# Separate PSUM banks for the two halves of one down-projection pair, two tail loads in place of one, and new engine orders, in a pre-norm linear-attention and GEGLU block

## The chip, the core and the metric

The kernel runs on one core of a Trainium2 chip. The metric is device time in microseconds (us), the median of repeated runs. One more execution was taken with the hardware profiler; its rows are quoted with the names the profile uses: PE is TensorE (PEld its weight loads), DVE VectorE, ACT ScalarE, POOL GpSimd, and SP SyncE, which here only issues DMAs.

## What is computed

One block of a transformer on x of 2048 rows by 448 columns in bfloat16: linear attention with 16 heads of 28, then a gated MLP of inner width 1792, each behind a layer norm and added to its input.

```
x = A_x;  h  = x + A(layernorm(x));  h2 = h + B(layernorm(h))
A: q, k, v = split(x @ wqkv);  phi(t) = where(t > 0, t + 1, exp(t)) + 1e-6
   kv = sum_s phi(k) v^T;  z = sum_s phi(k);  o = phi(q) kv / (phi(q) z + 1e-6);  return o @ wo
B: return (gelu(x @ w_gate) * (x @ w_up)) @ w_down
```

## The kernel before

**Tiles and stages.** The rows are cut into 16 tiles of 128, two tiles make a pair. The contraction over 448 columns is done as three blocks of 128 rows and a tail of 64 rows, padded with zeros to 128 (memsets, L364).

*Stage one*: for each tile, layer-norm statistics on DVE (`bnst1_t` L412, `bnag1_t` L413), the reciprocal root on ACT (`ln1_t` L419, `rstd1_t` L421), the normalised tile (`normD_t` L434 on DVE for tiles 0 to 3, `normP_t` L452 on POOL for the others), its transpose (for tiles 0 to 3 on PE, `tr0_t` and `tr1_t` L442, copied out of PSUM by ACT L447 and DVE, `evxD_t` L449; for the others a DMA transpose, L454), and the projections `k_t` and `q_t` (four matmuls each, L468; the fourth contracts the tail block). `k_t` is followed by `ek_t` (ACT, L479), `ck_t` (DVE, L480), `pk_t` (DVE, L481, the last reader of the projection's bank) and the accumulation `pt_t` (L487). The projections go round four PSUM banks in the order of the list SEQ (K0 K1 Q0 K2 K3 Q1 ...): `q_1` gets the bank of `k_1`, so it waits for `pk_1`.

*Stage two* makes the attention's output for each pair (`a2_pair`): some DVE and POOL work, a DMA transpose `oT`, the matmuls `outA`/`outB` (L626, L627), the residual, the second layer norm, a copy `wrap_t` on DVE (L663) that writes the tile a second time beside itself, and a DMA transpose `hT_t` issued by SP (L664).

*Stage three* is the MLP. `gu2_v` (chunks of two tiles) and `gu4_v` (chunks of four) are 28 or 14 matmuls of gate (L725) and up (L727); they contract 64 rows each, so that the two run at once in the upper and the lower half of the PE rows. ACT applies gelu (`ge0_v`, `ge1_v`, L745), DVE multiplies (`hm0_v`, `hm1_v`, L747). The first four-tile chunk, tiles 4 to 7, begins with `gu4_14` and needs `hT_4` to `hT_7`. The down projection of a pair (`b2_pair`, L695) is in two halves of 28 matmuls, `downA_p` and `downB_p`, which also contract 64 rows: in A tile a uses the upper 64 rows of PE and tile a+1 the lower, in B the other way. Both halves accumulate into the same two PSUM banks, 2 and 3, and B waits until A is done (`sync=parts[-1:]`). DVE adds the residual (`fo448_t`, L701) and SP stores the tile (`do_t`, L702). The last two tiles, 14 and 15, go through `b2_tile` (L677, matmuls over 128 rows, residual L681, store L682): tile 14 whole (`down448_14`), tile 15 in two halves of 224 columns (`down224_15`, twice).

**Order.** Nothing is scheduled at run time. Every operation is a task with a number (in order of creation); ORDERS is a list written out for each of the five instruction streams, in which the tasks are issued, and HOLD only says which of several waits of a task is put last. Waits on semaphores are derived from buffers; an engine whose next task must wait holds up all that stand behind it in its list.

**Loads.** `dma` (L346) issues on one of two queues, SP's and ACT's. Before, ACT issues x of tile 1, the three K blocks of wqkv (`dw0`), and the tail rows for K and Q together (`dw0_t`, 64 rows of 1792 bytes, buffer `b_wt`, read by every `k_t` and `q_t` with the fourth matmul). SP issues x of tiles 0 and 2 to 3, the Q blocks (`dw1`), x of tiles 4 to 7 (`dx4`), 8 to 11, 12 to 15, then V and wo.

Of the kernel before, what the change touches and what calls it, by code (L numbers as in the profile page):

```python
# [7 lines left out]
ALU = mybir.AluOpType  # L8
# [4 lines left out]


ORDERS = (
# [33 lines left out]
)  # L49
HOLD = {  # L50
    65: (35,), 140: (139,), 164: (163,), 213: (212,), 215: (214,), 322: (301,), 325: (323,), 430: (339,), 703:
    (563,), 734: (733,), 780: (671,), 838: (835,), 848: (845,),
}


# [173 lines left out]
def bass_sequential_preLN__linear_attn_block__glu_gated_geglu__prompt_kernel(  # L229
    nc, A_x, A_wqkv, A_wo, B_x, B_w_gate, B_w_up, B_w_down, out  # L230
):
    S, D, FF, H, DH = 2048, 448, 1792, 16, 28
    T, P = S // 128, S // 256
# [3 lines left out]
    NJ = FF // 128  # L237
# [11 lines left out]
    with es:  # L249
# [5 lines left out]
        x_sb = sb("x_sb", [128, T, D], BF16)  # L255
        xnn = sb("xnn", [128, XN_R, 512], BF16)
        xnT = sb("xnT", [128, T, 4, 128], BF16)
        wqk_sb = sb("wqk_sb", [128, 4, 2 * D], BF16)
# [3 lines left out]
        wd_sb = sb("wd_sb", [128, NJ, D], BF16)  # L262
# [25 lines left out]
        t1 = sb("t1", [128, 2, D], F32)  # L288
# [7 lines left out]
        hh = sb("hh", [128, NJ, HR * 128], BF16)  # L296
# [4 lines left out]
        ps = es.enter_context(nc.psum_tensor("ps", [128, 8, 512], F32))  # L301
# [5 lines left out]
        b_x = bufs("x", T)  # L307
        b_xn = bufs("xn", XN_R)
        b_xnT = [bufs("xnT%d_" % t, 2) for t in range(T)]
        b_ones2 = _Buf("ones2")  # L310
        b_wq, b_wk, b_wv = bufs("wq", 2), bufs("wk", 2), bufs("wv", 2)
        b_wpad = bufs("wpad", 2)
        b_wt = _Buf("wt")
        b_wo, b_wg, b_wu, b_wd = _Buf("wo"), bufs("wg", 2), bufs("wu", 2), _Buf("wd")
        b_ident, b_ones, b_mones, b_mtmp, b_mask, b_eps, b_mhalf, b_powtmp = (
            _Buf(n) for n in ("ident", "ones", "mones", "mtmp", "mask", "eps", "mhalf", "powtmp"))
# [6 lines left out]
        b_t1, b_den, b_rd = bufs("t1", 2), bufs("den", 4), bufs("rd", 4)  # L323
# [5 lines left out]
        b_ps = bufs("ps", 8)  # L329
# [5 lines left out]
        BK_KV, BK_W2 = 4, (5, 6, 7, 4)  # L335
        BK_TO, BK_OUT, BK_TH = (6, 7), (5, 4), (6, 7)
        BK_G, BK_U, BK_O = (0, 1), (6, 7), (2, 3)
        BK_L = {T - 2: (4,), T - 1: (5, 2)}

        xv = A_x[0].rearrange("(p t) d -> p t d", t=T)  # L340
        outv = out[0].rearrange("(p t) d -> p t d", t=T)
# [3 lines left out]
        def dma(q, out_ap, in_ap, w, name, r=(), after=()):  # L345
            t_ = G.add(q, lambda e: e.dma_start(out_ap, in_ap), r=r, w=w, name=name, kind="dma", after=list(after) + last[q])  # L346
            last[q] = [t_]
            return t_

        def op(eng, fn, r, w, name, after=()):  # L350
            return G.add(eng, fn, r=r, w=w, name=name, after=after)
# [4 lines left out]
        def dma_w1(q, dst, c0, c1, b, name):  # L356
            return dma(q, dst[A_, 3, c0 % (2 * D):c0 % (2 * D) + c1 - c0], A_wqkv[384:448, c0:c1], [b[1]], name)


        def dma_x(q, a, b):  # L360
            return dma(q, x_sb[:, a:b, :], xv[:, a:b, :], b_x[a:b], "dx%d" % a)
# [4 lines left out]
        dma_x("act", 1, 2)  # L366
        dma_x("sp", 2, 4)
        dma_w3("act", wqk_sb, D, 2 * D, b_wk, "dw0")
        tx1 = dma("act", wqk_sb[A_, 3, :], A_wqkv[384:448, 0:2 * D], [b_wt], "dw0_t")
        dma_w3("sp", wqk_sb, 0, D, b_wq, "dw1")  # L370
        dma_x("sp", 4, 8)
        dma_x("sp", 8, 12)
        dma_x("sp", 12, 16)
        dma_w3("sp", wv_sb, 2 * D, 3 * D, b_wv, "dwv")
# [94 lines left out]
            return ins  # L469

        def proj_reads(t, b):
            return [(b_xnT[t][0], 0), (b_xnT[t][1], 2), (b[0], 0), (b_wt, 3), (b_wpad[0], 3)]

        def k_tile(t):
            bk = slot()
# [207 lines left out]

        def b2_pair(p):
            a = 2 * p
            sl = [slice((t % HR) * 128, (t % HR + 1) * 128) for t in (a, a + 1)]
            parts = []
            for half in range(2):
                def fdp(e, W, half=half):
                    ins = None  # L690
                    for j in range(NJ):
                        W(j)
                        for n in range(2):
                            rows = (A_, B_)[(n + half) % 2]
                            ins = e.matmul(ps[:, BK_O[n], 0:D], hh[rows, j, sl[n]], wd_sb[rows, j, :], start=(half == 0 and j == 0), stop=(half == 1 and j == NJ - 1))  # L695
                    return ins
                parts.append(G.add("pe", fdp, r=[(b_ar[j][t % HR], j if j >= NJ - 2 else 0) for j in range(NJ) for t in (a, a + 1)] + [b_wd],
                                   w=[b_ps[b_] for b_ in BK_O], name="down%s_%d" % ("AB"[half], p), mw=True, sync=parts[-1:]))
            for n, t in enumerate((a, a + 1)):
                psO = ps[:, BK_O[n], 0:D]  # L700
                op("dve", lambda e, t=t, psO=psO: e.tensor_tensor(x_sb[:, t, :], psO, x_sb[:, t, :], ALU.add), [b_ps[BK_O[n]], b_x[t]], [b_x[t]], "fo448_%d" % t)  # L701
                G.add("sp", lambda e, t=t: e.dma_start(outv[:, t, :], x_sb[:, t, :]), r=[b_x[t]], name="do_%d" % t, kind="dma_out")  # L702

        vcount = [0]
# [112 lines left out]
```

## Time and profile before

| | us |
|---|---|
| median of 3 runs | 191.33 (190.81 to 191.39) |
| the profiled execution | 190.7 |
| its span, first to last instruction | 188.9 |
| PE busy in the span | 184.3 |
| DVE busy | 127.8 |

The span is what the profile's rows cover; the profiled execution's own time is 1.8 us longer. Times in rows are from the start of the span. A row of the timeline gives start, duration, engine, line, operation, output<-input and count, and in square brackets the idle time ahead of it with what ended it; consecutive instructions of a line are merged into one row. A row "issues" of the DMA view gives size and the time from issue to landing.

### The profile page before, as it was taken

The page shows a single profiled execution, that of the slowest core. Times are in us where ns is not written, and L with a number is a line of the kernel's source. Part 1 is how long each engine was busy: PE and PEld are TensorE (multiplying, and loading weights), DVE is VectorE, ACT ScalarE, POOL GpSimd, SP SyncE. Part 2 cuts the span into 40 slices and gives each one's busy share as a digit, 9 for nine tenths or more (in the row PEclk, how much of TensorE's full clock was granted, in tenths as well). Part 3 has the DMA queues.
Part 4 walks back from the last instruction along what each step waited for, and adds up shares of the span by engine and source line. Part 5 has one row for each costly group of instructions (what it writes and reads, how often), then busy time and mean ns, then how long its engine had stood idle before and what let it go on. Part 6 is the DMA issues. An engine that isn't in the chain of part 4 may idle for free.

```text
span 188.9 us, 4454 instructions
## 1 busy us (share of the span) xinstructions
PE 184.3 (98%) x1813; PEld 108.4 (57%) x1813; DVE 127.8 (68%) x328; ACT 76.4 (40%) x220; POOL 50.0 (26%) x91
## 2 busy tenths in 40 slices
PE   7799999999999999999999999999999999999994
PEld 7355555555688788965555555545545545454643
DVE  4999859999899998786796762562744343345232
ACT  3778752799963231432234222222142222324100
POOL 5067920604405686023614000207100000000000
PEclk9999999999999999999999999999999999999999
DMA  5985558999493525920005720000095000001025
GB/s 174 384 226 80 94 113 174 222 217 189 61 323 64 97 52 112 88 52 0 0 3 97 144 53 0 0 3 2 8 153 87 3 0 24 3 0 49 3 83 184
DMA packets 34996, 17.11 MB, mean 91 GB/s; under 512 B 26848, under 2 KB 33568, under 8 KB 34976
## 3 DMA queue, kind: packets, MB, share of 16 engines
q1 hardware_dynamic: 34352, 16.26, 41.4%
q10 hardware_dynamic: 624, 0.57, 0.9%
q8 instruction: 14, 0.23, 0.5%
q14 instruction: 6, 0.05, 0.1%
HBM read 8.26 MB, written 1.84 MB: 53 GB/s over the span
## 4 chain that ended last, share of the span: by engine, by line
PE 93%; DMA 3%; DVE 2%; ACTq 0%; issue 0%
PE ps L727 38%; PE ps L695 19%; PE ps L468 12%; PE ps L725 9%; PE ps L487 6%; DMA wqk_sb<-in_A_wqkv_dram 3%; PE ps L677 3%; PE ps L626 3%; PE ps L627 2%; PE ps L616 1%; PE ps L546 1%; PE ps L526 1%; ACTq L346 0%; PE ps L653 0%; DVE den L571 0%; DVE pt_sb L515 0%
## 5 line engine op out<-in xcount | busy, mean ns | idle before, releaser
L727 PE MATMUL ps<-hnT,wgu_sb 64*128 64x512 bf16 (+1 forms) x490 | 88.8, 333 | 0.0
L725 PE MATMUL ps<-hnT,wgu_sb 64*128 64x512 bf16 (+1 forms) x490 | 88.6, 333 | 0.0
L745 ACT ACTIVATE gl<-ps 128x256 bf16<-128x256 f32 x112 | 36.6, 383 | 85.3 <-PE ps L725 84.4
L747 DVE TENSOR_TENSOR hh<-ps,gl 128x256 bf16<-128x256 f32 x112 | 42.1, 416 | 41.5 <-ACT gl L745 41.4
L727 PEld LDWEIGHTS ps<-hnT,wgu_sb 64*128 64x128 bf16 x490 | 45.2, 94 | 32.9 <-DVE hh L747 3.4
L725 PEld LDWEIGHTS ps<-hnT,wgu_sb 64*128 64x128 bf16 x490 | 45.5, 94 | 2.6
L695 PE MATMUL ps<-wd_sb,hh 64*128 64x448 bf16 x392 | 41.7, 349 | 0.0
L695 PEld LDWEIGHTS ps<-wd_sb,hh 64*128 64x128 bf16 x392 | 22.7, 94 | 14.9 <-issue 0.2
L468 PE MATMUL ps<-wqk_sb,xnT 128*128 128x448 bf16 x128 | 27.5, 353 | 0.2 <-DMA wqk_sb<-in_A_wqkv_dram 0.2
L412 DVE BATCH_NORM_STATS2 st<-x_sb 128x6 f32<-128x448 bf16 x32 | 19.2, 612 | 1.8 <-DMA x_sb<-in_A_x_dram 1.7
L468 PEld LDWEIGHTS ps<-wqk_sb,xnT 128*128 128x128 bf16 x128 | 12.2, 98 | 11.7 <-DMA wqk_sb<-in_A_wqkv_dram 0.5
L584 POOL TENSOR_TENSOR t<-pq,zbc 128x448 f32<-128x448 bf16 x12 | 12.3, 1042 | 23.7 <-DVE pq L582 22.0
L487 PE MATMUL ps<-pk,xnn 128*128 128x448 bf16 x64 | 13.9, 352 | 0.0
L701 DVE TENSOR_TENSOR x_sb<-ps,x_sb 128x448 bf16<-128x448 f32 x14 | 8.5, 617 | 5.4 <-PE ps L695 5.4
L626 PE MATMUL ps<-w,pqnT 64*128 64x448 bf16 x49 | 11.5, 349 | 0.1
L424 POOL TENSOR_SCALAR ln<-mv 128x2 f32<-128x2 f32 x7 | 2.0, 290 | 35.2 <-DVE mv L413 35.0
L479 ACT ACTIVATE e<-ps 128x448 bf16<-128x448 f32 x16 | 8.5, 539 | 6.1 <-PE ps L468 5.9
L627 PE MATMUL ps<-pt_sb,pqnT 64*128 64x448 bf16 x42 | 10.2, 350 | 0.0
L632 DVE TENSOR_TENSOR x_sb<-ps,x_sb 128x448 bf16<-128x448 f32 x16 | 9.6, 616 | 0.7 <-PE ps L627 0.6
L661 POOL TENSOR_SCALAR hn<-x_sb,nm,rs 128x448 bf16<-128x448 bf16 x14 | 9.9, 719 | 0.4
L481 DVE SCALAR_TENSOR_TENSOR pk<-ps,e 128x448 bf16<-128x448 f32 x16 | 9.8, 617 | 0.1
L487 PEld LDWEIGHTS ps<-pk,xnn 128*128 128x128 bf16 x64 | 6.3, 98 | 5.8 <-DVE pk L481 0.3
(83 smaller groups left out, 158.4 us busy)
## 6 DMA issues: line engine op xcount, KB each, us to landing
out_dram<-x_sb SPq DMA_DIRECT2D x15, 112.0 KB, 1.8
wd_sb<-in_B_w_down_dram SPq DMA_DIRECT2D x1, 1568.0 KB, 8.3
x_sb<-in_A_x_dram SPq DMA_DIRECT2D x3, 448.0 KB, 6.5
wgu_sb<-in_B_w_gate_dram SPq DMA_DIRECT2D x1, 896.0 KB, 12.2
wgu_sb<-in_B_w_up_dram SPq DMA_DIRECT2D x1, 896.0 KB, 16.5
wgu_sb<-in_B_w_gate_dram SPq DMA_DIRECT2D x1, 672.0 KB, 6.1
wgu_sb<-in_B_w_up_dram SPq DMA_DIRECT2D x1, 672.0 KB, 8.6
wo_sb<-in_A_wo_dram SPq DMA_DIRECT2D x1, 392.0 KB, 8.2
```

The source lines that it names most:

```text
L412: op("dve", lambda e: e.bn_stats(st[:, t, :], src_ap), [b_src], [b_st[t]], "bnst%s_%d" % (tag, t))
L468: ins = e.matmul(ps[:, bk, 0:D], xnT[:, t, k, :], wqk_sb[:, k, c0:c0 + D], start=(k == 0), stop=(k == 3))
L487: ins = e.matmul(ps[:, BK_PT[c], 0:D], xnn[:, t % XN_R, c * 128:(c + 1) * 128], pk[:, ip, :], start=(t == 0), stop=(t == T - 1))
L584: op("pool", lambda e, n=n: e.tensor_tensor(t1[:, n, :], pq[:, a + n, :], zbc[:, :], ALU.mult), [b_pq[a + n]] + b_z, [b_t1[n]], "t1p_%d" % ...
L626: e.matmul(ps[:, BK_OUT[0], 0:D], pqnT[ra, i2, sg // 2, :], w2[ra, sg // 2, :], start=(sg == 0), stop=(sg == 5))
L627: ins = e.matmul(ps[:, BK_OUT[1], 0:D], pqnT[rb, i2, 3 + (sg + 1) // 2, :], (w2 if sg == 6 else w2s)[rb, sg // 2, :], start=(sg == 0), sto ...
L661: op("pool", lambda e, t=t, sh=sh: e.tensor_scalar(hn[:, sh, 0:D], x_sb[:, t, :], nm2[:, t:t + 1], rs2[:, t:t + 1], ALU.add, ALU.mult), [b ...
L695: ins = e.matmul(ps[:, BK_O[n], 0:D], hh[rows, j, sl[n]], wd_sb[rows, j, :], start=(half == 0 and j == 0), stop=(half == 1 and j == NJ - 1))
L725: first = e.matmul(psG[:, jj * N:(jj + 1) * N], wgu_sb[A_, k, j * 128:(j + 1) * 128], hnT[A_, ka_, c0:c0 + N], start=(k == 0), stop=(k == ...
L727: ins = e.matmul(psU[:, jj * N:(jj + 1) * N], wgu_sb[B_, k, j * 128:(j + 1) * 128], hnT[B_, kb_, c0:c0 + N], start=(k == 0), stop=(k == NK ...
L745: G.add("act", lambda e, gi=gi, cs_=cs_, psG=psG: e.activation(gl[:, gi, cs_], psG[:, cs_], AF.Gelu_apprx_tanh), r=[b_ps[BK_G[i]]], w=[b_g ...
L747: op("dve", lambda e, dst=dst, srcU=srcU, srcL=srcL: e.tensor_tensor(dst, srcU, srcL, ALU.mult), [b_ps[BK_U[i]], b_glh], [b_ar[j_][t % HR] ...
```

## The change

Three things are changed.

1. **Pair six** (tiles 12 and 13): `downA_6` accumulates into banks 4 and 5, `downB_6` into banks 2 and 3, each half a group of its own, and B no longer waits for A. DVE adds the A half and the residual into a float32 tile (`fa448_t`, new), then the B half to that (`fo448_t`). Tiles 14 and 15 get other banks: 1, and 7 and 0.
2. **Tail rows of wqkv**: ACT's queue loads only K's (64 rows of 896 bytes, still `dw0_t`). Q's are a load of their own on SP's queue (`dw1_t`), behind x of tiles 4 to 7 and ahead of tiles 8 to 11. `k_t` reads only K's and `q_t` only Q's.
3. **All five orders** are written anew (the numbers move by one or more, as tasks are added). At the places that the text below speaks of, they read:

| where | before | after |
|---|---|---|
| PE, start | `tr0_0 tr1_0 tr0_1 tr1_1 k_0`, `tr_2 k_1 q_0 tr_3 k_2 k_3 pt_0 q_1` | `tr1_0 tr0_0 tr0_1 tr1_1 k_0`, `tr_2 k_1 tr_3 k_2 q_0 k_3 pt_0 q_1` |
| DVE, start | `bnst1_0 bnag1_0 bnst1_1 bnag1_1 normD_0 bnst1_2 normD_1` | `bnst1_0 bnst1_1 bnag1_0 bnag1_1 bnst1_2 normD_0 bnag1_2 normD_1` |
| DVE, middle | `fo448_1 wrap_7 hm0_9 wrap_6 hm1_9` | `wrap_7 hm0_9 hm1_9 fo448_1 hm1_10 wrap_6` |
| PE, middle | `outA_4 gu2_11 outB_4 gu2_12 gu2_13 gu4_14` | `gu2_11 outA_4 gu2_12 outB_4 gu2_13 gu4_14` |
| PE, end | `downA_6 down224_15 downB_6 down448_14 down224_15` | `downA_6 downB_6 down224_15 down224_15 down448_14` |
| SP, end | `do_15 do_4 do_0 do_12 do_3 do_6 do_2 do_13 do_10 do_14 do_7 do_15` | `do_13 do_0 do_12 do_10 do_6 do_8 do_15 do_7 do_15 do_3 do_4 do_14` |

The diff, without the lists of numbers:

```diff
-        BK_L = {T - 2: (4,), T - 1: (5, 2)}
+        BK_L = {T - 2: (1,), T - 1: (7, 0)}
+        BK_O6 = ((4, 5), (2, 3))
...
-        tx1 = dma("act", wqk_sb[A_, 3, :], A_wqkv[384:448, 0:2 * D], [b_wt], "dw0_t")
+        tx1 = dma_w1("act", wqk_sb, D, 2 * D, b_wk, "dw0_t")
         dma_w3("sp", wqk_sb, 0, D, b_wq, "dw1")
         dma_x("sp", 4, 8)
+        dma_w1("sp", wqk_sb, 0, D, b_wq, "dw1_t")
         dma_x("sp", 8, 12)
...
-            return [(b_xnT[t][0], 0), (b_xnT[t][1], 2), (b[0], 0), (b_wt, 3), (b_wpad[0], 3)]
+            return [(b_xnT[t][0], 0), (b_xnT[t][1], 2), (b[0], 0), (b[1], 3), (b_wpad[0], 3)]
...
         def b2_pair(p):
             a = 2 * p
+            bko = BK_O6 if p == 6 else (BK_O, BK_O)
...
-                            ins = e.matmul(ps[:, BK_O[n], 0:D], hh[rows, j, sl[n]], wd_sb[rows, j, :], start=(half == 0 and j == 0), stop=(half == 1 and j == NJ - 1))
+                            ins = e.matmul(ps[:, bko[half][n], 0:D], hh[rows, j, sl[n]], wd_sb[rows, j, :], start=(j == 0 and (half == 0 or p == 6)), stop=(j == NJ - 1 and (half == 1 or p == 6)))
...
-                                   w=[b_ps[b_] for b_ in BK_O], name="down%s_%d" % ("AB"[half], p), mw=True, sync=parts[-1:]))
+                                   w=[b_ps[b_] for b_ in bko[half]], name="down%s_%d" % ("AB"[half], p), mw=True, sync=parts[-1:] if p != 6 else []))
             for n, t in enumerate((a, a + 1)):
-                psO = ps[:, BK_O[n], 0:D]
-                op("dve", lambda e, t=t, psO=psO: e.tensor_tensor(x_sb[:, t, :], psO, x_sb[:, t, :], ALU.add), [b_ps[BK_O[n]], b_x[t]], [b_x[t]], "fo448_%d" % t)
+                psO = ps[:, bko[1][n], 0:D]
+                xt, bx = x_sb[:, t, :], b_x[t]
+                if p == 6:
+                    xt, bx = t1[:, n, :], b_t1[n]
+                    op("dve", lambda e, t=t, n=n: e.tensor_tensor(t1[:, n, :], ps[:, bko[0][n], 0:D], x_sb[:, t, :], ALU.add), [b_ps[bko[0][n]], b_x[t]], [b_t1[n]], "fa448_%d" % t)
+                op("dve", lambda e, t=t, psO=psO, xt=xt: e.tensor_tensor(x_sb[:, t, :], psO, xt, ALU.add), [b_ps[bko[1][n]], b_x[t], bx], [b_x[t]], "fo448_%d" % t)
```

More of the change, by code (lines that the diff above doesn't have):

```diff
@@ L15 @@
 ORDERS = (
[33 rows of a table removed]
[33 rows of a table added]
 )
 HOLD = {
-    65: (35,), 140: (139,), 164: (163,), 213: (212,), 215: (214,), 322: (301,), 325: (323,), 430: (339,), 703:
-    (563,), 734: (733,), 780: (671,), 838: (835,), 848: (845,),
+    66: (36,), 141: (140,), 305: (298,), 323: (302,), 498: (378,), 565: (427,), 704: (564,), 725: (724,), 837:
+    (836,), 849: (846,), 857: (852,), 866: (865,),
 }
@@ L312, in bass_sequential_preLN__linear_attn_block__glu_gated_geglu__prompt_kernel @@
         b_wpad = bufs("wpad", 2)
-        b_wt = _Buf("wt")
         b_wo, b_wg, b_wu, b_wd = _Buf("wo"), bufs("wg", 2), bufs("wu", 2), _Buf("wd")
```

66 rows, old and new, of the table ORDERS are left out of this document.

## The prediction

> **What bounds the kernel now.** First the busy times and the chain on the page, then the busy time by stretches, to see where PE stands still.
>
> ```profile
> PE 184.3 (98%) x1813; PEld 108.4 (57%) x1813; DVE 127.8 (68%) x328; ACT 76.4 (40%) x220; POOL 50.0 (26%) x91
> ...
> PE 93%; DMA 3%; DVE 2%; ACTq 0%; issue 0%
> ```
>
> ```profile
> 0.00:7.83 7.83, 5.78 (x55) 4.64 (x56) 4.98 (x16) 3.91 (x11) 2.82 (x11) 1.00 0.77 254
> 7.83:36.30 28.47, 28.44 (x156) 14.54 (x153) 25.17 (x73) 18.72 (x55) 13.65 (x31) 1.00 0.74 162
> 36.30:50.50 14.20, 14.11 (x107) 8.09 (x109) 13.69 (x33) 13.77 (x36) 4.59 (x5) 1.00 0.90 168
> 50.50:175.00 124.50, 124.50 (x1401) 74.32 (x1399) 80.35 (x200) 39.31 (x119) 28.92 (x46) 1.00 0.30 55
> 175.00:188.90 13.90, 11.44 (x103) 6.80 (x97) 3.65 (x8) 0.66 (x2) 0.00 (x0) 0.99 0.28 92
> ```
>
> In a row of the stretches the second number is the length; then come PE, its weight loads, DVE, ACT, POOL, the granted clock, the DMA share and GB/s. From 7.83 to 175 us PE is busy 167.05 of 167.17 us at full clock. The change takes no matmul away, so this middle can't become shorter; it can only open gaps. What can be won lies ahead of 7.83 us and behind 175 us.
>
> **The start.** Two views: the timeline of PE, then of DVE.
>
> ```profile
> 6.32 0.92 PE L468 MATMUL ps<-wqk_sb,xnT 128*128 128x448 bf16 x3
> 7.46 0.36 PE L468 MATMUL ps<-wqk_sb,xnT 128*128 128x448 bf16 x1 [0.23 <-DMA wqk_sb<-in_A_wqkv_dram]
> ...
> 11.89 0.92 PE L468 MATMUL ps<-wqk_sb,xnT 128*128 128x448 bf16 x4
> ```
>
> ```profile
> 5.11 0.62 DVE L412 BATCH_NORM_STATS2 st<-x_sb 128x6 f32<-128x448 bf16 x1
> 5.64 0.38 DVE L434 TENSOR_SCALAR xnn<-x_sb,mv,rs 128x448 bf16<-128x448 bf16 x1
> ...
> 6.03 0.59 DVE L412 BATCH_NORM_STATS2 st<-x_sb 128x6 f32<-128x448 bf16 x1
> 6.54 0.27 DVE L449 COPY xnT<-ps 128x256 bf16<-128x256 bf16 x1
> ...
> 8.29 0.62 DVE L412 BATCH_NORM_STATS2 st<-x_sb 128x6 f32<-128x448 bf16 x1
> ...
> 11.20 0.60 DVE L481 SCALAR_TENSOR_TENSOR pk<-ps,e 128x448 bf16<-128x448 f32 x1
> 11.72 0.17 DVE L413 BATCH_NORM_AGGREGATE mv<-st 128x2 f32<-128x6 f32 x1
> ```
>
> ```profile
> x_sb<-in_A_x_dram SPq DMA_DIRECT2D x1, 448.0 KB, 5.9
> wqk_sb<-in_A_wqkv_dram ACTq DMA_DIRECT2D x1, 112.0 KB, 5.7
> ```
>
> The first two rows are `k_0`: its third matmul starts at 6.32 + 0.92 - 0.36 = 6.88, and the fourth could follow 0.19 later ((0.92 - 0.36) / 3 in the third row), at 7.07. It starts at 7.46, when the 112 KB tail has landed: **0.39 us lost**. With 56 KB the tail should come sooner. By how much shows in what the packets of ACT's queue cost:
>
> ```profile
> q10 hardware_dynamic: 512, 0.43, 47.3%
> ...
> q10 hardware_dynamic: 80, 0.11, 18.2%
> ```
>
> The first row is 2.0 to 4.7 us, packets of 896 bytes: 0.473 x 16 engines x 2.7 us / 512 = 0.040 us each. The second is 5.3 to 7.0 us, 64 tail packets of 1792 bytes and 16 end marks: 4.95 us in all, about 0.077 for a tail packet. Each engine has four of them, so halving their size saves at least 4 x 0.037 = 0.15 us, and more where one shared its engine with a large x packet. The Trainium skill (DMA: Bandwidth & Descriptors, Measured) holds that "Transfers under 64 KB are descriptor-dominated"; by that the tail of 56 KB would land no sooner and nothing would be won at `k_0`. The two rows say that half the bytes take half the time, so I don't go by it.
>
> But PE keeps this only if what follows is ready. `bnag1_0` now stands behind `bnst1_1`, and `normD_0` behind `bnst1_2` (5.64 - 5.11 = 0.53 us from its start to the next): tile 0 is normalised up to 0.53 later. That is covered up to the copy `evxD_0` at 6.54, which stood behind `bnst1_3` (6.03) anyway, so the third matmul of `k_0` hardly moves, from 6.88 to about 6.9. Then comes the next bound. From 8.29 on DVE goes on without a pause through `pk_1`, which ends at 11.80; `q_1`, which takes the bank of `pk_1`, starts at 11.89. The 8.29 is `bnst1_4`, which needs x of tiles 4 to 7, issued at 2.17 and landed 5.9 later, at 8.07. So the DVE chain to `q_1` gains at most 8.29 - 8.07 = 0.22, and the new order puts one more short instruction, `bnag1_6`, ahead of `pk_1` (0.17 in the last row). With the 0.09 of slack at `q_1`, 11.89 - 11.80, that leaves 0.22 - 0.17 + 0.09 = 0.14 of the 0.39. **I take 0.15 gained.** Its ends: 0.39 if x of tiles 4 to 7 comes earlier too (56 KB less goes ahead of it), 0.1 lost if the tail stays where it is.
>
> The tail for Q stands on SP's queue behind x of tiles 4 to 7 and should land soon after 8.07; `q_0` needs it with its fourth matmul, now behind `k_1` and `k_2`, not before 7.3 + 2 x 0.76 + 0.57 = 9.4. I cost it at nothing; the cover is 1.3 us, and if that is gone PE waits for the rest. It puts one SP issue ahead of x of tiles 8 to 15 and 56 KB on their queue; the first use of them, `bnst1_8`, comes behind the last DVE row above, so that too is hidden.
>
> **The end.** PE, DVE and SP from 175 us, from three timelines, and three issues.
>
> ```profile
> 175.12 3.02 PE L695 MATMUL ps<-wd_sb,hh 64*128 64x448 bf16 x28
> 178.07 1.51 PE L677 MATMUL ps<-wd_sb,hh 128*128 128x224 bf16 x14
> 179.52 2.82 PE L695 MATMUL ps<-wd_sb,hh 64*128 64x448 bf16 x28
> 182.28 4.16 PE L677 MATMUL ps<-wd_sb,hh 128*128 128x448 bf16 x28
> ```
>
> ```profile
> 182.38 1.15 DVE L701 TENSOR_TENSOR x_sb<-ps,x_sb 128x448 bf16<-128x448 f32 x2 [2.37 <-PE ps L695]
> 185.13 0.62 DVE L681 TENSOR_TENSOR x_sb<-ps,x_sb 128x448 bf16<-128x448 f32 x1 [1.60 <-PE ps L677]
> 186.47 0.39 DVE L681 TENSOR_TENSOR x_sb<-ps,x_sb 128x224 bf16<-128x224 f32 x1 [0.72 <-PE ps L677]
> ```
>
> ```profile
> 185.87 0.45 SPq L682 DMA_DIRECT2D out_dram<-x_sb  x1
> 186.37 0.45 SPq L702 DMA_DIRECT2D out_dram<-x_sb  x1
> 186.89 0.41 SPq L682 DMA_DIRECT2D out_dram<-x_sb  x1
> ```
>
> ```profile
> 64.04 2.65 PE ps L695 x28
> ```
>
> ```profile
> out_dram<-x_sb SPq DMA_DIRECT2D x1, 112.0 KB, 1.8
> out_dram<-x_sb SPq DMA_DIRECT2D x1, 56.0 KB, 1.6
> ```
>
> Half a pair takes 2.65 when nothing disturbs it (the row at 64.04); 14 matmuls of 224 columns take half as long as 14 of 448, 1.34. So the three changes between matmuls over 64 and over 128 rows cost 178.07 - 177.77 = 0.30, 179.52 - 179.41 = 0.11 and 182.28 - 182.17 = 0.11. In the new order A and B of pair six follow each other and all of tiles 14 and 15 comes behind: one change is left, of the first kind. **0.22 gained** on PE. But tile 14 is now last, whole: its residual takes 0.62 and not 0.39, **0.23 lost**, and its store of 112 KB lands in 1.8 and not 1.6 us, **0.2 lost**. PE's gain is eaten by what comes behind PE. The two `fa448` lie beside `downB_6`; DVE is busy 3.65 of the last 13.9 us, and about 1.2 more is hidden (at nothing).
>
> SP has no slack here. `do_13` can go at about 181.45 (B of pair six starts at 177.77, its residual 2.86 later as from 179.52 to 182.38, and takes 0.62, plus up to 0.2 as the two row halves of PE end 0.2 apart), and 11 stores behind it at 0.49 each (185.87 to 186.37) put `do_14` at 186.85, as late as its data.
>
> **The middle.** PE's 124.5 us stay covered if every input of the gate and up matmuls is in time. The tightest is `gu4_14`, which needs `hT_4` to `hT_7`.
>
> ```profile
> 81.17 0.38 PE L725 MATMUL ps<-hnT,wgu_sb 64*128 64x512 bf16 x1
> ```
>
> ```profile
> 74.03 2.64 SPq L664 DMA_TRANSPOSE hnT<-hn  x2
> ```
>
> ```profile
> hnT<-hn SPq DMA_TRANSPOSE x14, 3.0
> ...
> q14 instruction: 1, 0.01, 4.5%
> q8 instruction: 1, 0.02, 2.6%
> ...
> hnT<-hn SPq DMA_TRANSPOSE x1, 5.1
> ```
>
> The two transposes are `hT_7` (74.03) and `hT_6` (75.30). 3.0 is the median to landing; `hT_6` took 5.1 (the last rows are 76.3 to 78.5 us), as two instruction blocks were loaded in that time, and landed at 80.4, 0.7 ahead of PE. In the new order `wrap_6` stands behind `hm1_10`, which waits for `gu2_10` and gelu: about 76.3, and so `hT_6` is issued **1.0 later**. It lands at 79.3 with 3.0, at 81.4 with 5.1; PE comes at 81.17 - 0.15 = 81.0. So the wait is 0 to 0.4. The nearest row is `hT_6` itself: what held it up passes at its own time, so a later issue should shorten the delay. **I take 0.1 lost.** The Trainium skill (Runtime: NRT & Kernel Launch, Instruction fetch mechanics) calls the crossing of an instruction block "mostly hidden"; by it `hT_6` lands at 79.3 and the sum below is 0.1 less. The 5.1 speaks against that.
>
> **Sum.** -0.15 (start) + 0.1 (`gu4_14`) - 0.22 + 0.23 + 0.2 (end) = +0.16 us on the profiled execution's 190.7. The median of the runs is 191.33, 0.6 above that execution; with the same difference it becomes **191.5 us**.
>
> **Rivals.** (1) *A late `hT_6`, slower than before.* The block loads now fall into the data of `hT_7` and `hT_6` both. From a landing at 81.0 on, each microsecond costs one; if both are held up one after the other, at 2.1 each, `hT_6` lands near 82.5: 1.5 lost and not 0.1, **192.9**. For it: both were slow before (4.9 on average). Against it: one delay passed for both. (2) *New waits on PE.* All orders differ, and hm, fo and hr are interleaved anew with DVE 80.35 of 124.5 us busy; two or three late products at 0.2 to 0.4 each give **192.2**. (3) *The whole start is kept*: x of tiles 4 to 7 lands sooner, 0.39 gained, no wait at `gu4_14`, and the last store no slower than a half one: -0.39 - 0.22 + 0.23 = -0.4, **190.9**. For it: ACT's queue brings 56 KB less ahead of that load. Against it: the DVE rows between 8.29 and 11.80 leave no pause to close. (4) *Pair six doesn't do what it says*: B swaps the row halves, and PE drains between A and B although the banks differ, 0.2 as in the changes above: **191.7**.
>
> **Chances.** Forecast 0.48, (4) 0.07, (1) 0.15, (2) 0.15, (3) 0.15. About 0.3% (0.57 us) is what a measurement can tell from no change, so 190.76 to 191.90 counts as the same. The forecast and (4) lie inside. Of (3), 0.15 above the lower bound, about 0.08 falls outside by the spread of the runs (0.58). (1) and (2) lie outside, but for a small part. So faster 0.08, same 0.64, slower 0.28. The range takes the open ends: 0.39 kept and no wait below, 0.1 lost at the start, 0.4 at `gu4_14` and one late product above: 190.8 to 192.3. The far part of (1) and (2) and the faster tail of (3) are left out.
>
> **What would show it.** Right: the fourth matmul of `k_0` no longer idle before, `q_1` ended by DVE's L481 and starting 0.1 to 0.2 earlier; in the stretch to 175 us PE still busy throughout, with at most some tenths ahead of the first 64x512 matmul, ended by DMA; one gap in place of three behind the last gate matmul; the last DVE row 0.62 long, over 128x448. Wrong: the tail still landing near 7.4; idle before L725 or L727 that DVE ended; a store on SP issued later than its data.

## The result and the profile after

The changed kernel takes **191.44 us** (median of 22 runs, 191.12 to 191.83); the kernel before, in runs beside it, 191.06 (190.79 to 191.53). The ratio is **1.0016, 95% interval 1.0008 to 1.0023**: slower by 0.3 us, half of what counts as a difference here. The forecast was 191.5. The profiled execution of the changed kernel took 191.37, its span is 189.4 (before 190.7 and 188.9).

First the page's busy times and chain, then the stretches, of the changed kernel.

```profile
PE 184.8 (98%) x1813; PEld 120.0 (63%) x1813; DVE 129.2 (68%) x330; ACT 76.0 (40%) x220; POOL 50.0 (26%) x91
...
PE 93%; DVE 2%; DMA 2%; issue 0%; ACT 0%; SPq 0%
```

```profile
0.00:7.83 7.83, 6.22 (x56) 5.40 (x57) 4.92 (x16) 3.59 (x11) 3.06 (x10) 1.00 0.78 245
...
50.50:175.00 124.50, 124.50 (x1397) 84.63 (x1395) 79.49 (x199) 39.41 (x119) 29.12 (x46) 1.00 0.28 54
175.00:189.40 14.40, 11.57 (x105) 7.41 (x101) 5.34 (x11) 0.66 (x2) 0.00 (x0) 1.00 0.29 97
```

PE's share is the same as before (that of its weight loads rose, from 57% to 63%), and PE reads busy for all of 124.50 us in the middle, as before. But it did 1397 matmuls there and not 1401. The busy time hides the loss: matmuls in the two row halves overlap, so while one half waits the other, or a matmul still on its way out, keeps the column full. To see a loss, take the start of the first gate or up matmul and that of `downA_6` from PE's timeline. Before they stand at 50.50 (the row below, of the kernel before) and 175.12, and 124.62 us lie between them. In the changed kernel they are the first two rows of the second fence:

```profile
50.50 0.27 PE L727 MATMUL ps<-hnT,wgu_sb 64*128 64x256 bf16 x1
```

```profile
50.49 0.27 PE L733 MATMUL ps<-hnT,wgu_sb 64*128 64x256 bf16 x1
...
175.47 5.67 PE L697 MATMUL ps<-wd_sb,hh 64*128 64x448 bf16 x56
181.07 5.50 PE L678 MATMUL ps<-wd_sb,hh 128*128 128x224 bf16 x42
```

124.98 us: **the middle lost 0.36**. Where it lost, PE's timeline shows near 62 us, and its weight loads near 62 and 75.5:

```profile
61.61 0.35 PE L628 MATMUL ps<-w,pqnT 64*128 64x448 bf16 x1
61.74 0.27 PE L731 MATMUL ps<-hnT,wgu_sb 64*128 64x256 bf16 x1
62.00 0.28 PE L733 MATMUL ps<-hnT,wgu_sb 64*128 64x256 bf16 x1
```

```profile
62.00 0.09 PEld L733 LDWEIGHTS ps<-hnT,wgu_sb 64*128 64x128 bf16 x1 [0.35 <-DVE hh L753]
...
75.67 0.09 PEld L733 LDWEIGHTS ps<-hnT,wgu_sb 64*128 64x128 bf16 x1 [0.27 <-DVE hh L753]
```

L731 is gate and L733 up. The first gate matmul of `gu2_6` starts at 61.74, its up matmul should follow half a step (0.055) later and comes at 62.00. Both times the one that held it was a DVE product (L753) that reads the up bank to be written: `hm0_4` for `gu2_6`, `hm1_9` for `gu2_11`. DVE's timeline says why they were late:

```profile
59.89 0.33 DVE L664 COPY hn<-hn 128x448 bf16<-128x448 bf16 x1 [0.59 <-POOL hn L662]
60.15 0.61 DVE L633 TENSOR_TENSOR x_sb<-ps,x_sb 128x448 bf16<-128x448 f32 x1
60.68 0.61 DVE L413 BATCH_NORM_STATS2 st<-x_sb 128x6 f32<-128x448 bf16 x1
61.21 0.73 DVE L753 TENSOR_TENSOR hh<-ps,gl 128x256 bf16<-128x256 f32 x2
...
74.67 0.28 DVE L664 COPY hn<-hn 128x448 bf16<-128x448 bf16 x1 [1.98 <-POOL hn L662]
74.86 0.75 DVE L753 TENSOR_TENSOR hh<-ps,gl 128x256 bf16<-128x256 f32 x2
```

Each time DVE stands still ahead of a copy `wrap` that waits for POOL, with the two products queued behind it, the first time behind a residual and statistics as well. `hm1_4` and `hm0_4` end at 61.94, `hm1_9` at 75.61. The second time PE's new list has a part in it: with `gu2_11` ahead of `outA_4` the matmul that waits was due at 75.52, 0.5 earlier than the first of `gu2_11` in the kernel before (76.02), where `hm1_9` had ended at 75.28:

```profile
74.87 0.41 DVE L747 TENSOR_TENSOR hh<-ps,gl 128x256 bf16<-128x256 f32 x1
```

**The start.** PE, then DVE, of the changed kernel.

```profile
5.80 0.83 PE L443 MATMUL ps<-ident,xnn 128*128 128x128 bf16 x8 [0.28 <-DVE xnn L435]
6.88 0.93 PE L469 MATMUL ps<-wqk_sb,xnT 128*128 128x448 bf16 x4 [0.25 <-ACT xnT L448]
...
11.88 0.92 PE L469 MATMUL ps<-wqk_sb,xnT 128*128 128x448 bf16 x4
```

```profile
4.82 0.63 DVE L413 BATCH_NORM_STATS2 st<-x_sb 128x6 f32<-128x448 bf16 x1
5.36 0.38 DVE L435 TENSOR_SCALAR xnn<-x_sb,mv,rs 128x448 bf16<-128x448 bf16 x1
...
8.25 0.63 DVE L413 BATCH_NORM_STATS2 st<-x_sb 128x6 f32<-128x448 bf16 x1
...
11.19 0.62 DVE L482 SCALAR_TENSOR_TENSOR pk<-ps,e 128x448 bf16<-128x448 f32 x1
```

The four matmuls of `k_0` now run in one row: the fourth waits for no load. But the row begins at 6.88 and not at 6.32, as `normD_0` starts at 5.36 behind `bnst1_2`; before it started at 4.83:

```profile
4.83 0.36 DVE L434 TENSOR_SCALAR xnn<-x_sb,mv,rs 128x448 bf16<-128x448 bf16 x1
```

So `k_0` ends where it did, and `q_1` starts at 11.88 (before 11.89), behind a `pk_1` that ends at 11.81 (before 11.80). **In this profile the start gained nothing.**

**The end.** In PE's rows above, pair six runs in one piece of 56 matmuls, and one change to 128 rows is left: 181.07 - 175.47 = 5.60, two halves of 2.65 and 0.30. The three fences below are DVE's last row, SP's last row, and the issue that this is.

```profile
186.61 0.62 DVE L682 TENSOR_TENSOR x_sb<-ps,x_sb 128x448 bf16<-128x448 f32 x1 [2.26 <-PE ps L678]
```

```profile
187.26 0.33 SPq L683 DMA_DIRECT2D out_dram<-x_sb  x1
```

```profile
out_dram<-x_sb SPq DMA_DIRECT2D x1, 112.0 KB, 1.7
```

From the start of `downA_6` to that of the last DVE row it takes 186.61 - 175.47 = 11.14, before 186.47 - 175.12 = 11.35: 0.21 won on PE. The row itself is 0.62 and not 0.39: 0.23 lost. SP issues the store as soon as that row ends (187.23), so its list is not in the way. The store takes 1.7 and not 1.6.

0 (start) + 0.36 - 0.21 + 0.23 + 0.1 = +0.5 us; the spans differ by 0.5, the medians by 0.4.

### The profile page after: what moved, and what is told of

It reads as the page before. It is cut to its first block, busy times and chain, and to the rows that moved or that the text cites. A ratio compares the mean times of both kernels' runs of the same rounds, so it can differ in the third digit from the quotient of the medians.

```text
span 189.4 us, 4465 instructions
## 1 busy us (share of the span) xinstructions
PE 184.8 (98%) x1813; PEld 120.0 (63%) x1813; DVE 129.2 (68%) x330; ACT 76.0 (40%) x220; POOL 50.0 (26%) x91
## 4 chain that ended last, share of the span: by engine, by line
PE 93%; DVE 2%; DMA 2%; issue 0%; ACT 0%; SPq 0%
PE ps L733 38%; PE ps L697 19%; PE ps L469 12%; PE ps L731 8%; PE ps L488 6%; PE ps L627 3%; PE ps L678 3%; PE ps L628 2%; DMA x_sb<-in_A_x_dram 2%; PE ps L617 1%; PE ps L547 1%; PE ps L443 1%; PE ps L527 1%; PE ps L654 0%; DVE st L413 0%; DVE x_sb L682 0%
## 5 line engine op out<-in xcount | busy, mean ns | idle before, releaser
L733 PE MATMUL ps<-hnT,wgu_sb 64*128 64x512 bf16 (+1 forms) x490 | 89.1, 333 | 0.0
L731 PE MATMUL ps<-hnT,wgu_sb 64*128 64x512 bf16 (+1 forms) x490 | 89.1, 333 | 0.0
L753 DVE TENSOR_TENSOR hh<-ps,gl 128x256 bf16<-128x256 f32 x112 | 42.6, 416 | 35.7 <-ACT gl L751 35.5
L733 PEld LDWEIGHTS ps<-hnT,wgu_sb 64*128 64x128 bf16 x490 | 45.3, 94 | 26.4 <-DVE hh L753 2.9
L731 PEld LDWEIGHTS ps<-hnT,wgu_sb 64*128 64x128 bf16 x490 | 45.4, 94 | 3.1 <-DVE hnT L660 0.2
L697 PEld LDWEIGHTS ps<-wd_sb,hh 64*128 64x128 bf16 x392 | 26.1, 94 | 11.5
L585 POOL TENSOR_TENSOR t<-pq,zbc 128x448 f32<-128x448 bf16 x12 | 13.1, 1106 | 17.0 <-DVE pq L583 14.9
L417 POOL TENSOR_SCALAR nm<-mv 128x1 f32<-128x1 f32 (+1 forms) x19 | 4.3, 230 | 39.1 <-DVE mv L414 38.6
L633 DVE TENSOR_TENSOR x_sb<-ps,x_sb 128x448 bf16<-128x448 f32 x16 | 9.6, 612 | 1.6 <-PE ps L628 1.6
L453 POOL TENSOR_SCALAR xnn<-x_sb,nm,rs 128x448 bf16<-128x448 bf16 x12 | 8.9, 741 | 4.0 <-ACT rs L422 4.0
```

Of the source, the lines that this page charges most:

```text
L585: op("pool", lambda e, n=n: e.tensor_tensor(t1[:, n, :], pq[:, a + n, :], zbc[:, :], ALU.mult), [b_pq[a + n]] + b_z, [b_t1[n]], "t1p_%d" % ...
L697: ins = e.matmul(ps[:, bko[half][n], 0:D], hh[rows, j, sl[n]], wd_sb[rows, j, :], start=(j == 0 and (half == 0 or p == 6)), stop=(j == NJ ...
L731: first = e.matmul(psG[:, jj * N:(jj + 1) * N], wgu_sb[A_, k, j * 128:(j + 1) * 128], hnT[A_, ka_, c0:c0 + N], start=(k == 0), stop=(k == ...
L733: ins = e.matmul(psU[:, jj * N:(jj + 1) * N], wgu_sb[B_, k, j * 128:(j + 1) * 128], hnT[B_, kb_, c0:c0 + N], start=(k == 0), stop=(k == NK ...
L753: op("dve", lambda e, dst=dst, srcU=srcU, srcL=srcL: e.tensor_tensor(dst, srcU, srcL, ALU.mult), [b_ps[BK_U[i]], b_glh], [b_ar[j_][t % HR] ...
```

## The experiments

Each ratio is against the kernel before, run beside it on the same chip, with its 95% interval. It is not the quotient of the two medians, from which it differs by up to 0.15 us. The difference of two rows carries the intervals of both, 0.25 to 0.35 us either way, so a tenth or two between two kernels is not a finding by itself.

| kernel | median us | kernel before | ratio |
|---|---|---|---|
| changed | 191.44 | 191.06 | 1.0016 [1.0008, 1.0023] |
| changed, middle mended | 190.91 | 191.00 | 1.0001 [0.9990, 1.0012] |
| changed, a half tile last | 190.84 | 191.00 | 1.0000 [0.9990, 1.0011] |
| changed, start order of before | 191.28 | 191.00 | 1.0015 [1.0005, 1.0025] |
| before, split tails alone | 190.93 | 191.00 | 0.9995 [0.9979, 1.0011] |
| changed, middle mended and half last | 190.52 | 191.04 | 0.9965 [0.9951, 0.9978] |
| before, pair six alone | 190.66 | 191.04 | 0.9979 [0.9967, 0.9990] |
| before, both parts | 190.75 | 191.04 | 0.9983 [0.9971, 0.9996] |
| before, both parts, start anew | 191.03 | 191.04 | 0.9993 [0.9980, 1.0007] |
| changed, one tail again | 191.36 | 190.93 | 1.0015 [1.0005, 1.0026] |
| changed, all three mended | 190.48 | 190.93 | 0.9976 [0.9967, 0.9986] |

### The middle mended

Four products are moved in DVE's list:

```
- wrap_2 hr_4 bnst2_5 hm1_4 hm0_4 wrap_3 ... hm0_8 wrap_7 hm0_9 hm1_9 fo448_1
+ wrap_2 hr_4 hm1_4 hm0_4 bnst2_5 wrap_3 ... hm0_8 hm0_9 hm1_9 wrap_7 fo448_1
```

> The changed kernel with four DVE products moved: hm1_4 and hm0_4 now ahead of bnst2_5 (behind hr_4), hm0_9 and hm1_9 ahead of wrap_7. Theory: the middle lost 0.35 us because two up matmuls (of gu2_6 near 62 us and of gu2_11 near 75.5 us) waited for the product that reads their bank; with the products earlier both gaps (0.16 each) close, PE is busy to within 0.1 us from 50.5 to 175 us, and the time falls 0.3 us against the changed kernel, to 0 to +0.1 us against the kernel before. Rival: the gaps only move, since hr_4 and bnst2_5 or the transposed tiles are late in turn: less than 0.1 us gained, and another matmul waits.

1.0001 against 1.0016: 0.29 us gained, just clear of the intervals (0.25). PE's timeline of this kernel, first matmul of the MLP and `downA_6`:

```profile
50.62 0.27 PE L733 MATMUL ps<-hnT,wgu_sb 64*128 64x256 bf16 x1
...
175.25 0.94 PE L697 MATMUL ps<-wd_sb,hh 64*128 64x448 bf16 x7
```

124.63 us lie between them, as before the change (124.62). The stretch again counts 1401 matmuls:

```profile
50.50:175.00 124.50, 124.50 (x1401) 81.40 (x1399) 80.01 (x199) 39.51 (x119) 29.14 (x46) 1.00 0.29 54
```

So the loss in the middle is the place of four products in DVE's list, with PE's list as it is now, and no other wait costs PE time in their stead.

### A half tile last

```
- PE:  downA_6 downB_6 down224_15 down224_15 down448_14
+ PE:  downA_6 downB_6 down224_15 down448_14 down224_15
- DVE: fo448_12 fo224_15 fo224_15 fo448_14
+ DVE: fo448_12 fo224_15 fo448_14 fo224_15
- SP:  do_5 do_9 do_11 do_13 do_0 do_12 do_10 do_6 do_8 do_15 do_7 do_15 do_3 do_4 do_14
+ SP:  do_5 do_9 do_11 do_0 do_10 do_6 do_8 do_7 do_3 do_4 do_13 do_12 do_15 do_14 do_15
```

> The changed kernel with its end in the old manner: down448_14 between the two down224_15, so that a half of tile 15 (128x224) is last, and the stores whose rows are long done ahead of do_13 on SP. Pair six keeps its four banks. Theory: tile 14 last and whole cost 0.23 us of residual and 0.06 us of store; the last DVE row becomes 0.39 long, PE keeps its 0.21, and the time falls 0.25 to 0.3 us against the changed kernel. Rival: SP, which spends 0.49 us on a store, sends the last one behind do_14 and not as soon as its data are there: less than 0.1 us gained.

1.0000: 0.3 us gained, as the first theory has it. DVE's last row of this kernel, and its last store:

```profile
186.37 0.39 DVE L682 TENSOR_TENSOR x_sb<-ps,x_sb 128x224 bf16<-128x224 f32 x1 [0.72 <-PE ps L678]
```

```profile
out_dram<-x_sb SPq DMA_DIRECT2D x1, 56.0 KB, 1.5
```

The gain is just clear of the intervals, too. SP's list was changed with it, so the two aren't told apart; what the run shows is that a half last does not make SP the bound.

### The start in the order of before

```
- DVE: bnst1_0 bnst1_1 bnag1_0 bnag1_1 bnst1_2 normD_0 bnag1_2 normD_1
+ DVE: bnst1_0 bnag1_0 bnst1_1 bnag1_1 normD_0 bnst1_2 normD_1 bnag1_2
- ACT: ln1_2 evxA_0
+ ACT: evxA_0 ln1_2
- PE:  tr1_0 tr0_0, tr1_2 tr0_2
+ PE:  tr0_0 tr1_0, tr0_2 tr1_2
```

> The changed kernel with the order of the start as before (bnag1_0 ahead of bnst1_1, normD_0 ahead of bnst1_2, normD_1 ahead of bnag1_2 on DVE; evxA_0 ahead of ln1_2 on ACT; tr0 ahead of tr1 on PE); both tails stay split. Theory: k_0 starts at 6.3 and not 6.88, its fourth matmul follows at 7.1, but x of tiles 4 to 7 still lands at 8.2 and the DVE chain to pk_1 still ends at 11.8, so PE loses at q_1 (or at k_3, whose xnT comes by evxD_3 in the same chain) what it won: within 0.1 us of the changed kernel. Rival: the order alone ate the gain of the tail, and the time falls 0.3 us.

1.0015 against 1.0016: no difference, although PE's timeline shows `k_0` at 6.30, 0.58 earlier:

```profile
6.30 1.11 PE L469 MATMUL ps<-wqk_sb,xnT 128*128 128x448 bf16 x4
...
11.66 0.93 PE L469 MATMUL ps<-wqk_sb,xnT 128*128 128x448 bf16 x4
```

Only 0.22 of that is left at `q_1` (11.66 for 11.88). DVE's timeline shows `bnst1_4` at 8.04, when x of tiles 4 to 7 had landed, 5.8 us after its issue (6.1 in the changed kernel's profile):

```profile
8.04 0.63 DVE L413 BATCH_NORM_STATS2 st<-x_sb 128x6 f32<-128x448 bf16 x1
```

```profile
x_sb<-in_A_x_dram SPq DMA_DIRECT2D x1, 448.0 KB, 5.8
```

From `bnst1_4` to `q_1` it is 11.66 - 8.04 = 3.62, in the changed kernel 11.88 - 8.25 = 3.63, before 11.89 - 8.29 = 3.60. So the way to `q_1` does go by that chain. The 0.22 lies within what profiles of one and the same start scatter by: the kernel with a half tile last has the start of the changed kernel, and there `q_1` starts at 11.63.

### The split tails alone, on the kernel before

```
- ACT: dw0_t = 64 rows of K and Q, 112 KB
+ ACT: dw0_t = 64 rows of K, 56 KB;  SP: dw1_t = 64 rows of Q, behind dx4
```

> The kernel before with only the tail rows of K and Q split (Q's behind x of tiles 4 to 7 on SP), all orders as before. Theory: the tail for K lands near 7.1 in place of 7.41 and k_0 no longer waits for it, but the time stays within 0.1 us of the kernel before, because q_1 goes by the DVE chain that starts with x of tiles 4 to 7. Rival, the prediction's own term: 0.15 us faster, or up to 0.39 if that load comes sooner as well.

0.9995, interval 0.9979 to 1.0011: 0.1 us faster, and anything from 0.4 faster to 0.2 slower. By itself this tells neither theory from the other. The load did what it was to do: it landed 5.3 after its issue and `k_0` ran through, in PE's timeline:

```profile
wqk_sb<-in_A_wqkv_dram ACTq DMA_DIRECT2D x1, 56.0 KB, 5.3
```

```profile
6.39 1.11 PE L467 MATMUL ps<-wqk_sb,xnT 128*128 128x448 bf16 x4
```

### Middle mended and half last together

The edits of the first two experiments.

> The changed kernel with both repairs together: the four products of gu2_6 and gu2_11 earlier, and a half of tile 15 last with SP's stores in the order of their data. Theory: the two costs lie in different stages and on PE's own path, so they add up: 0.6 us under the changed kernel, 0.2 to 0.3 us under the kernel before (ratio near 0.9987), PE in the profile busy but for 0.1 us from 50.5 to 175 us and the last DVE row 0.39 long. Rival: what was won in the middle waits again behind it (a transposed tile or a store), and only one of the two shows: ratio 1.000.

0.9965 (0.9951 to 0.9978, five runs of this kernel): 0.7 us under the kernel before (0.5 by the medians), 1.0 under the changed one. The gains add up. It is more than the 0.6 expected; the sum of the two single ones, 1.0016 - 0.0015 - 0.0016 = 0.9985, carries the intervals of three ratios, so the rest isn't a finding.

### Pair six alone, on the kernel before

The edits of `b2_pair` and of the banks, and

```
- PE: downA_6 down224_15 downB_6 down448_14 down224_15
+ PE: downA_6 downB_6 down224_15 down448_14 down224_15
```

The ends of DVE's and SP's lists are changed to match; SP's stores go in a new order.

> The kernel before with only pair six in four banks and added in float32 (downA_6, downB_6, half of tile 15, tile 14, half of tile 15), one tail as before, and all orders ahead of the end as before. Theory: two of three changes between matmuls over 64 and 128 rows go, 0.2 us off PE's end, and what comes behind PE stays 0.39 and 1.6 long: 0.2 us under the kernel before. Rival: the residual and the store behind PE set the end by another bound (SP's stores 0.5 us apart): no difference.

0.9979: faster, by 0.2 to 0.6 us, where 0.2 was expected. In PE's timeline of this kernel the pair is one row, and one change is left, 180.85 - 175.25 - 5.30 = 0.30:

```profile
175.25 5.67 PE L696 MATMUL ps<-wd_sb,hh 64*128 64x448 bf16 x56
180.85 5.51 PE L677 MATMUL ps<-wd_sb,hh 128*128 128x224 bf16 x42
```

### Both parts, orders of before

> Both parts of the change with the orders of the kernel before: tails split as in the change, pair six in four banks, a half of tile 15 last; DVE, ACT, PE and POOL ahead of the end as before. Theory: what the change costs beside these two parts is its orders; here there is no wait in the middle, k_0 is not late, and the end is 0.2 us shorter: 0.2 us (tail worth nothing) to 0.4 us (tail worth 0.2) under the kernel before. Its difference from the pair alone is what the split tails are worth. Rival: the split tails cost as much as they win (one more load on SP ahead of x of tiles 8 to 15): no faster than the pair alone.

0.9983 against 0.9979 for the pair alone: the split tails add nothing that shows (0.1 us slower, and 0.3 either way). In PE's timeline of this kernel a new wait stands at `k_6`, for the DMA transpose of tile 6:

```profile
17.92 0.92 PE L468 MATMUL ps<-wqk_sb,xnT 128*128 128x448 bf16 x4 [0.16 <-DMA xnT<-xnn]
```

The kernel with the split tails alone has the same lists up to the end, and in its profile PE does not wait there.

### The same with the start ordered anew

```
- DVE: normD_3 evxD_2 bnst1_4 ck_0 bnag1_4 bnst1_5 pk_0 bnag1_5 evxD_3 ck_1 bnst1_6 pk_1
+ DVE: evxD_2 normD_3 ck_0 bnst1_4 evxD_3 bnag1_4 pk_0 ck_1 bnst1_5 pk_1 ck_2 bnag1_5 bnst1_6
```

The lists of ACT, POOL and PE for stage one are changed to match. `bnst1_4` and `bnst1_5` still stand ahead of `pk_1`.

> As both parts with the old orders, and the start ordered anew, so that the way to q_1 no longer starts with x of tiles 4 to 7: on DVE evxD_3, pk_0, ck_1 and pk_1 go ahead of the statistics of tiles 5 and 6, with ACT, POOL and PE's order of the first tiles to match. Theory: what held the gain of the tail back is the DVE chain behind x of tiles 4 to 7; with these out of the way q_1 starts 0.2 to 0.3 us earlier and PE keeps it to the end: 0.1 to 0.2 us under the kernel with the old orders, 0.4 to 0.6 us under the kernel before. Rival: the statistics put off are late for the norms and transposes of tiles 5 to 8, and PE waits for them near 15 to 20 us: no gain or a loss.

0.9993 against 0.9983 with the old orders: 0.2 us slower, which is inside the intervals (0.35). `q_1` starts no earlier than with the old orders (11.55 for 11.53), so the edit did not do what the theory asks of it. The profile goes the rival's way, with a wait at `k_5` in PE's timeline:

```profile
17.02 1.69 PE L468 MATMUL ps<-wqk_sb,xnT 128*128 128x448 bf16 x8 [0.77 <-DMA xnT<-xnn]
```

`bnst1_5` came 1 us later and with it the issue of tile 5's transpose. The transpose also took longer. DMA issues under way between 12.4 and 12.9 us, first of the kernel with the old orders, then of this one; both rows are tile 5's:

```profile
xnT<-xnn SPq DMA_TRANSPOSE x1, 2.5
```

```profile
xnT<-xnn SPq DMA_TRANSPOSE x1, 4.3
```

Behind `q_1` a third bound can come up, then: the transposed tiles 5 and 6. It does in the profiles of these two kernels alone.

### One tail again

The changed kernel with the load of 112 KB for K and Q back, all else as changed.

> The changed kernel with the tail rows of K and Q in one load of 112 KB again, all else as changed. Theory: the tail lands at 7.4 to 7.5 in place of 7.07, and it makes no difference, because q_1 and k_6 behind it go by x of tiles 4 to 7 and by the transposed tile 6 anyway: within 0.1 us of the changed kernel, ratio 1.0015 to 1.002 against the kernel before. Rival: the split was worth its 0.15 to 0.39 us and something else ate it: that much slower than the changed kernel, ratio 1.0024 to 1.0037.

1.0015 against 1.0016: no difference, though the interval (1.0005 to 1.0026) takes in the lower end of the rival's. The profiled execution happens to be the longest of eleven (191.81, with x of tiles 4 to 7 landing 6.7 after its issue), but it shows the wait that the split takes away, in PE's timeline:

```profile
6.53 0.84 PE L468 MATMUL ps<-wqk_sb,xnT 128*128 128x448 bf16 x3
7.78 0.36 PE L468 MATMUL ps<-wqk_sb,xnT 128*128 128x448 bf16 x1 [0.41 <-DMA wqk_sb<-in_A_wqkv_dram]
```

0.41 us of waiting at `k_0` come and go, and the median of the runs hardly moves (191.36 for 191.44).

### All three mended

> The changed kernel with the middle and the end mended and the start in the order of the kernel before. Theory: the start order alone made no difference (1.0015 against 1.0016), so nothing is added to the two repairs: ratio 0.9965 within 0.001. Rival: with the other losses gone, k_0 at 6.3 in place of 6.5 to 6.9 shows to the end: 0.2 to 0.3 us more, ratio near 0.995.

0.9976, just outside the band expected. Its median is 190.48, that of the two repairs 190.52: the start order adds nothing that shows. These two are faster than the kernel before, by 0.5 to 0.7 us, and than the changed one.

## Why the prediction was right, and where it was not

The time was right, 191.44 for 191.5, and of the signs "same" is what came. That it came so close is luck: the 191.5 starts from 191.33, the median of three runs, and 22 runs put the kernel before at 191.06, 0.27 lower; the sum said +0.16 and the medians say +0.38, 0.22 more. The two nearly cancel. (The range's lower end is wider than its own terms: 191.33 - 0.39 - 0.22 + 0.23 + 0.2 is 191.15, not 190.8.) The steps fared unequally.

**The end, PE: right.** 0.22 was forecast from the changes between 64 and 128 rows, 0.21 is in the trace, and pair six alone makes the kernel before faster. Rival (4), a drain between A and B, is out: the 56 matmuls are one row.

**The end, behind PE: right in kind, the store too large.** The residual cost the 0.23 forecast. The store cost 0.1 (1.7 for 1.6) and not 0.2: the 1.8 that I took is that of a store in the midst of others, not of the last one. The Trainium skill (DMA: Bandwidth & Descriptors, Measured) has it that "Transfers under 64 KB are descriptor-dominated"; the stores fit that, as the last one took 1.5 to 1.6 with 56 KB and 1.7 with 112 KB. Putting a half last gained 0.3 us, these two terms together. SP, which I said had no slack (at 0.49 a store; the rows give 0.50), held nothing up.

**The start: 0.15 forecast, and not seen.** The load came sooner, as forecast (5.3 after its issue, for 5.7; 4.9 to 5.3 in the nine profiles with 56 KB, 5.7 to 6.0 in the three with 112), and the fourth matmul of `k_0` no longer waits. But `q_1`, which was to start 0.1 to 0.2 earlier, did not. Three comparisons price the split itself: alone on the kernel before it is 0.1 faster, with pair six beside it 0.1 slower, and taken back from the changed kernel it makes 0.0, each with 0.25 to 0.3 either way. Together that is 0.0, and 0.2 either way: rival (3), with 0.39 kept, is out, while 0.15 is not excluded. What the twelve profiles say, from PE's timeline of each:

| start | kernel | `q_1` | first matmul of the MLP | between |
|---|---|---|---|---|
| one tail, order of before | before | 11.89 | 50.50 | 38.61 |
| | pair six alone | 12.02 | 50.63 | 38.61 |
| split, order of before | split tails alone | 11.58 | 50.20 | 38.62 |
| | both parts | 11.53 | 50.48 | 38.95 |
| split, new order but for the first tiles | start order of before | 11.66 | 50.27 | 38.61 |
| | all three mended | 11.76 | 50.37 | 38.61 |
| split, new order | changed | 11.88 | 50.49 | 38.61 |
| | middle mended | 12.01 | 50.62 | 38.61 |
| | a half tile last | 11.63 | 50.29 | 38.66 |
| | middle mended and half last | 11.89 | 50.51 | 38.62 |
| one tail, new order | one tail again | 12.50 | 51.12 | 38.62 |
| split, start anew | both parts, start anew | 11.55 | 51.11 | 39.56 |

From `q_1` to the MLP it is 38.6 in ten of the twelve: what is won or lost at `q_1` is kept to the MLP. The transposed tiles take it back in two kernels only, not in the changed one. So the bound that I named, the DVE chain from x of tiles 4 to 7 to `q_1`, is the last that counts in the changed kernel, and it is about as long as I counted: 3.63 from `bnst1_4` to `q_1`, where my terms make 3.60 + 0.17 - 0.09 = 3.68. What failed is its beginning. `bnst1_4` was to start at 8.07 and started at 8.25, as x of tiles 4 to 7 landed 6.1 after its issue, to the tenth, and not 5.9. In the four profiles with this start that load took 5.6 to 6.2, and `q_1` came between 11.63 and 12.01: 0.15 lies inside that scatter. With the lists of before, the split brings `q_1` 0.3 to 0.5 earlier, but the timed runs don't show that either. So the term isn't settled, beyond its lying below about 0.2.

The step "the third matmul of `k_0` hardly moves, from 6.88 to about 6.9" holds in three of the four profiles with the split and the new order (6.9 to 7.0 by the lengths of the rows). In that of the changed kernel it came at about 7.3, where x of tiles 2 and 3 had also landed late, 3.6 after its issue and not 3.1 to 3.4.

**The middle: the wrong place.** The 0.1 for `gu4_14` did not come. DMA issues of `hT_7` (first) and `hT_6` of the changed kernel, and the first gate matmul of `gu4_14` in PE's timeline:

```profile
hnT<-hn SPq DMA_TRANSPOSE x1, 4.7
```

```profile
hnT<-hn SPq DMA_TRANSPOSE x1, 3.6
```

```profile
81.48 0.38 PE L731 MATMUL ps<-hnT,wgu_sb 64*128 64x512 bf16 x1
```

`hT_6` went 1.4 later than before and landed at 80.3, 1.2 ahead of PE, so what had held it up passed at its own time, as I had it, and rival (1) is out; what it was, these runs don't tell. The 0.36 that was lost is rival (2): products behind other DVE work. It had 0.15 and a price of 0.7; two waits came, and not at 0.2 to 0.4 each but at 0.15 to 0.2. How little cover there was stands in DVE's timeline of the kernel before:

```profile
60.16 0.73 DVE L747 TENSOR_TENSOR hh<-ps,gl 128x256 bf16<-128x256 f32 x2
```

`hm0_4` and `hm1_4` ended at 60.89, 0.9 us before the up matmul of `gu2_6` is due (61.8). The new list puts the statistics ahead of them (0.53), and a copy whose wait for POOL was 0.59: they end 1.05 later, at 61.94, more than the cover, and the matmul comes 0.2 late. I weighed DVE by its share (80 of 124.5 us busy), where the place in its list decides.

So by the terms of the profiles the sum was 0.3 short: a gain not made at the start (0.15) and 0.26 more lost in the middle, against 0.1 less at the store. What the timed runs bear out clearly is the middle and the end: mended together they take the change from 0.3 us slower to 0.5 to 0.7 us faster.

## What to carry to other kernels

Where a list is written by hand, follow it task by task with the durations of the old trace wherever its engine waits for another one: four products behind copies that waited for POOL cost more than pair six gained on PE. A stage that reads 100% busy may still lose time: compare starts of the same work, or count instructions in the stretch. Before paying to take a wait away at the start of a chain, look for the next bound behind it. And look at what stands behind the last engine: the shorter piece goes last.

## What the runs showed of the hardware

- The same DMA transpose of a tile took 2.5 us when issued near 11.7 us and 4.3 when issued near 12.7. The next tile's, issued between 13.0 and 13.8, took 3.9 to 4.4 in eight of the profiles. What slows them was not tried.
- Issued at the same time in each execution, x of tiles 4 to 7 landed 5.6 to 6.7 us later in the twelve profiles, and the start moves with it. One profile per kernel can't settle a few tenths there; the timed runs had to.
- Two halves over 64 rows in different banks follow each other without a pause (56 matmuls in one row, two times 2.65); the change to 128 rows behind the second costs 0.30.
